# Denominators of two head pairs in one group of products, the key-query transposes of odd visits moved ahead of their scores, and another timetable for converting weights

## The chip, the cores and the metric

The kernel runs on one core of a Trainium2 chip. Its time is the device time of one execution in microseconds (us). The engines are named as in the profile: PE is TensorE (matrix products and transposes), PEld its loading of weights, DVE is VectorE, ACT is ScalarE, POOL is GpSimd, SP issues most DMAs. Each engine works through its own queue in order.

## The reference

```python
# q, k, v: (8, 12, 448, 64) f32; g_q, g_k: (64,); w_in: (768, 2048); w_out: (2048, 768)
def rmsnorm(x, g):
    return x / sqrt(mean(x * x, axis=-1) + 1e-6) * g
q_n, k_n = rmsnorm(q, g_q), rmsnorm(k, g_k)
scores = q_n @ k_n.T / 8
attn = exp(scores - max(scores)); attn = attn / (sum(attn) + 1e-9)
x = (attn @ v).transpose(0, 2, 1, 3).reshape(3584, 768)
h = maximum(x @ w_in, 0)
out = (h * h) @ w_out
```

## The kernel before

Two heads make a pair; a batch of 12 heads has 6 pairs, and 8 batches have 48, counted `i` = 0, 1, ... in order. Two pairs (an even one and the odd one behind it) share work: the 448 keys of a head are 3 slots of 128 keys and one of 64, and the last 64 keys of two pairs go together as slot `NJ` = 3.

The work around the change is **phase 1**, the visits of pairs 0 to 12 (`visit_alone(i, n)`, called for n = 0 and then n = 1). There PE does attention only. Behind it, PE's stream of FFN products begins (line L1016 first), with the attention of later pairs in between. The branch of the program used here is `shift` = False, in which exps need no shift by their maximum. Nothing is scheduled at run time: the order of instructions on every engine is that in which Python issues them, and semaphores do the waiting.

What a visit of pair i does before, by engine (lines of the kernel before):

- PE: scores of slots 0 and 1 of pair i (`score`, L449, products on 64x64 tiles, into banks 0 to 3); the **turn** of pair i+1 (`turn`, transposes of q and k by L415 and L418, q in bank 7 and k in bank 6); the values of pair i-1 for slots 0 to 2 (`attend`, L552, bank 4 for an even pair and 5 for an odd one); scores of slot 2 (L449, banks 0 and 1 again); then in an even visit the scores of the shared slot (L460, banks 2 and 3), in an odd visit the values of the shared slot for both pairs (`attend_both`, L588, the odd pair's half into bank 6); last the **sums**, the denominators of pair i-1, as products of the weights with ones (`add_weights`, L604, 16 products, four at a time side by side).
- ACT: the exps (L468) of the scores that make the weights; the squares of q (L181); the copy of k from its bank (L425); the copy of the odd pair's half, `rest` (L595); part of the conversion of FFN weights (L1696 to L1699).
- DVE: the **inversion** of pair i-2's denominators, which were summed at the end of the visit before: a transposition out of the bank (`take_sums`, L664), four small copies (L675), an addition (L676), a reciprocal (L681), a transposition back (L682); then `finish`: for an odd pair add `rest` (L715), multiply the values by the inverse (L717). For pairs of batch 1 `begin_forms` sums x into forms for the FFN (L744, on DVE and POOL in turn). Then qT of pair i+1 out of its bank (L423), and the means of squares of pair i+2, q and then k (L194, L197).
- POOL: squares of k of pair i+2 (L183), the power -1/2 of the means (L204), and the scaling of q (L219), which the next visit's turn of q waits for.
- The conversion of FFN weights: `convert` starts a piece (ACT, then DVE L1710 and L1729) at the steps in `early` (step 4i + 2n), and `make_sum` adds pieces to weight forms (L1810, one instruction on DVE, the next on POOL).

After phase 1 the sums of weights of pair 12 are added on POOL (L487) and multiplied with ones on PE (L622).

Of the kernel before, what the change touches and what calls it, by code (L numbers as in the profile page):

```python
# [14 lines left out]
F32 = mybir.dt.float32  # L15
# [4 lines left out]
ALU = mybir.AluOpType  # L20
# [3 lines left out]
P = 128  # L24


NJ = 3
NG = 2 * NJ + 1
SIDE = 32
# [196 lines left out]
def program(ctx, tc, rows, v, g, wide, ones, moe_w_in, moe_w_out, out, shift):  # L226

    nc = tc.nc

    B, H, S, D = v.shape  # L230
    NPAIR = H // 2
# [6 lines left out]
    NT = S // P  # L238
# [23 lines left out]
    banks = [psum.tile([P, 512], F32, name=f"bank{n}") for n in range(8)]  # L262
# [3 lines left out]
    pairs = [(b, c) for b in range(B) for c in range(NPAIR)]  # L266
    LASTS = S - NJ * P
# [141 lines left out]
    def turn(i, x):  # L409

        ensure("qk", i)
        tr = banks[7 - x if i < 2 or alone(i - 2) else 0]
        dst = att.tile([P, S], F32, name="qT" if x == 0 else "kT")
        for j in range(NJ):
            nc.tensor.transpose(  # L415
                tr[:, ts(j, P)], rows.part(i, x)[:, j].rearrange("p h d -> p (h d)"), ident
            )
        nc.tensor.transpose(  # L418
            tr[:, ts(NJ, P)], rows.room(i)[:, x, NJ].rearrange("p h d -> p (h d)"),
            wide[:, ds(i % 2 * LASTS, P)],  # L420
        )
        if x == 0:
            nc.vector.tensor_scalar(out=dst, in0=tr[:, 0:S], scalar1=g, scalar2=None, op0=ALU.mult)  # L423
        else:
            nc.scalar.copy(dst, tr[:, 0:S])  # L425
        turned[i, x] = dst

    def new_weights(n, e):

        i, m = n  # L430
        if m < 2 and alone(i) and not shift:
            weights[n, e] = new_acc()[:, 0:S] if m else new_part()
        else:
            weights[n, e] = att.tile([P, S], F32, name="wT", tag="wT", bufs=8)
        return weights[n, e]

    def banks_of(i, m):

# [90 lines left out]
    def values_bank(i):  # L529
        return banks[4 + i % 2 if alone(i) else 4][:, 0:S]  # L530

    def attend(i, some):

        order = values_of(i)
        for n in (i, i + 1 if i % 2 == 0 and not shift else i):
            ensure("v", n)
        for n in some:  # L540
            if n >= len(order):
                continue
            m = order[n]
            if m == NJ and not shift:
                attend_both(i)
                continue
            if joint(i):
                attend_halves(i, n)
                continue
            mine = ds(i % 2 * LASTS, LASTS) if m == NJ else ds(0, P)  # L550
            for e in range(2):
                nc.tensor.matmul(  # L552
                    values_bank(i)[ds(e * D, D), :],
                    lhsT=lasts[i % 2][mine, e, :] if m == NJ else values[i][:, m, e, :],
                    rhs=weights[key_of(i, m), e][mine], start=n == 0,
                    stop=n == len(order) - 1 and (shift or i % 2 == 1),
                )

    def second_bank(i):
        return banks[3][:, 0:S]  # L560
# [36 lines left out]
    def add_weights(i, some):  # L597

        order = sums_of(i)
        for n in some:  # L600
            m = order[n]
            mine = ds(i % 2 * LASTS, LASTS) if m == NJ and shift else ds(0, P)
            for e in range(2):
                nc.tensor.matmul(  # L604
                    sums_bank(i)[ds(e * D + n % 2 * SIDE, SIDE), :],
                    lhsT=ones_of[i % 2][mine] if m == NJ else ones[:, 0:SIDE],
                    rhs=weights[key_of(i, m), e][mine], start=n < 2, stop=n >= 2,
                )
# [53 lines left out]
    def take_sums(i):  # L662
        inverse[i] = io.tile([P, S], F32, name="inverse", tag="squares", bufs=1)
        nc.vector.transpose(inverse[i], sums_bank(i))  # L664
# [4 lines left out]
    def invert(i):  # L669
        columns = inverse[i].rearrange("p (t n) -> p t n", n=SIDE)  # L670
        few = columns[:, :, 0:1]
        if alone(i) or shift:
            other, both = new_few(), new_few()
            for n in range(P // SIDE):
                nc.vector.tensor_copy(out=other[ts(n, SIDE)], in_=few[ts(n ^ 1, SIDE)])  # L675
# [6 lines left out]
        nc.vector.transpose(columns, by.to_broadcast([P, S // SIDE, SIDE]))  # L682
# [22 lines left out]
    def finish(i):  # L705

        b, c = pairs[i]
        if joint(i):
            xT = xts[b, c]
            nc.gpsimd.tensor_tensor(out=xT, in0=xT, in1=inverse.pop(i), op=ALU.mult)  # L710
        else:
            xT = xts[b, c] = new_x()
            bank = values_bank(i)
            if i % 2 and not shift:
                nc.vector.tensor_tensor(out=xT, in0=bank, in1=rests.pop(i), op=ALU.add)  # L715
                bank = xT
            nc.vector.tensor_tensor(out=xT, in0=bank, in1=inverse.pop(i), op=ALU.mult)  # L717
        leave(i)

    def leave(i):  # L720
        b, c = pairs[i]
        scale_turned()
        for x in range(2):
            del turned[i, x]
        del values[i]
        if b == 1:
            begin_forms(c)
        elif b > 1:
            settle(b, c)
# [1129 lines left out]
    load_weights(1)  # L1859
    for i in range(2, 4):  # L1860
        rows.load(i, nc.sync)
    for n in range(2):
# [86 lines left out]
    def new_acc():  # L1949
        return keep_p.tile([P, DM], F32, name="acc", tag="acc", bufs=2 * NT + 1)  # L1950
# [30 lines left out]
    def visit_alone(i, n):  # L1981
        step = i * 2 * VISITS + 2 * n
        if n == 0:
            if i == 0:
                load_v(i)
            if i and shift:
                attend_all(i - 1)
            weigh_slots(i, n)
            turn(i + 1, 0)
            turn(i + 1, 1)  # L1990
            square(i + 2, 0, new_acc())
            square(i + 2, 1, new_acc(), nc.gpsimd)
            begin(step)
            normalize(i + 2, 0)
            if i and not shift:
                attend(i - 1, range(NJ))
        else:
            weigh_slots(i, n)
            normalize(i + 2, 1)
            begin(step)  # L2000
            if in_blocks(i + 2):
                store_q(i + 2)
                load_blocks(i + 2, 0)
                load_blocks(i + 2, 1)
            if i and not shift:
                attend(i - 1, (NJ,))
                add_weights(i - 1, range(NJ + 1))
                forget(i - 1, range(NJ + 1))
                take_sums(i - 1)
                invert(i - 1)  # L2010
                finish(i - 1)
            if i < 2 * NPAIR:
# [196 lines left out]
```

## Time and profile before

| | |
|---|---|
| median of 3 runs | 1348.09 us (1348.0 to 1348.48) |
| the profiled execution | 1348.26 us, its span 1346.5 us, TensorE clock granted 0.999 |
| phase 1 | about 17 us to 122.2 us of the span; 13 visits |
| an undisturbed visit | 8.40 us |

Busy time of the engines in stretches of the span; columns: stretch, its length, then busy time and instructions of PE, PEld, DVE, ACT, POOL, the granted clock, the DMA share and GB/s:

```profile
44.00:61.00 17.00, 17.00 (x144) 6.28 (x140) 15.21 (x37) 15.10 (x29) 12.46 (x11) 1.00 0.64 161
95.00:122.00 27.00, 25.59 (x212) 9.38 (x204) 23.46 (x50) 15.61 (x29) 19.11 (x17) 1.00 0.59 159
122.00:500.00 378.00, 376.12 (x1531) 185.44 (x1528) 280.90 (x494) 239.03 (x421) 248.28 (x213) 1.00 0.78 213
```

In a row of a timeline or of the chain the first number is the start in us from the span's start, the second the time in us. `x4` counts the instructions that the row gathers. In brackets stands how long the engine had been idle, and what released it. The visit of pair 9 starts at 87.08, that of pair 10 at 95.47, of pair 11 at 104.30, of pair 12 at 112.79. The FFN stream starts at 122.22.

### The profile page before, as it was taken

To read this page: it belongs to the slowest core of one execution; us is meant where nothing else is said; L and a number is where in the kernel's file an instruction comes from. 1 tells how busy PE (TensorE), PEld (TensorE's weight loads), DVE (VectorE), ACT (ScalarE), POOL (GpSimd) and SP (SyncE) were. 2 spreads that over 40 slices of the span, in tenths; PEclk is the share of its full clock that TensorE was granted. 3 is DMA by queue.
4 is the path that set the end of the run, shared out by engine and by line. 5 is a ranking of instruction groups with operands and counts; after the bars stand their busy time and mean duration, and the time that the engine had idled before them with its cause. 6 is when DMAs were issued, how large, how long until landed. Compare 5 with 4: busy or idle time off the path is not lost.

```text
span 1346.5 us, 21086 instructions
## 1 busy us (share of the span) xinstructions
PE 1326.0 (98%) x6988; PEld 887.2 (66%) x6988; DVE 884.0 (66%) x1739; ACT 611.4 (45%) x1135; POOL 760.6 (56%) x740
## 2 busy tenths in 40 slices
PE   7999999999999999999999999999999999999998
PEld 3333454444444486777758576676858599999998
DVE  4887866878768856465656856565655854556673
ACT  6885677768666244442434244353433134330000
POOL 5668764746556878566767878576555731110010
PEclk9999999999999999999999999999999999999999
DMA  5655965968969877574748676674737466545543
GB/s 137 156 142 131 247 187 144 283 182 219 266 149 268 255 189 221 154 219 124 234 104 251 190 186 211 169 214 119 238 83 231 145 194 196 157 132 152 161 158 101
DMA packets 416633, 245.64 MB, mean 182 GB/s; under 512 B 273284, under 2 KB 381060, under 8 KB 415492
## 3 DMA queue, kind: packets, MB, share of 16 engines
q1 hardware_dynamic: 416224, 244.15, 64.2%
q8 instruction: 57, 0.93, 0.3%
q14 instruction: 60, 0.49, 0.1%
q10 hardware_dynamic: 292, 0.07, 0.0%
HBM read 178.13 MB, written 65.99 MB: 181 GB/s over the span
## 4 chain that ended last, share of the span: by engine, by line
PE 90%; DVE 4%; DMA 2%; SPq 1%; POOL 1%; issue 1%; ACT 1%; POOLq 0%; DVEq 0%; ACTq 0%
PE bank L1077 26%; PE bank L1274 21%; PE bank L1600 9%; PE bank L1016 8%; PE bank L449 8%; PE bank L567 4%; PE bank L552 4%; PE bank L1438 2%; PE bank L460 1%; PE bank L588 1%; PE bank L604 1%; PE bank L1216 1%; PE bank L631 1%; PE bank L622 1%; DVE acc L1636 1%
## 5 line engine op out<-in xcount | busy, mean ns | idle before, releaser
L1077 PE MATMUL bank<-xT,in_sb 128*128 128x224 f32 x1344 | 287.0, 353 | 0.0
L1077 PEld LDWEIGHTS bank<-xT,in_sb 128*128 128x128 f32 x1344 | 253.1, 190 | 9.4 <-ACT wT L468 5.6
L468 ACT ACTIVATE wT<-bank,rr 128x448 f32<-128x448 f32 x288 | 163.8, 631 | 160.5 <-PE bank L449 134.9
L1274 PE MATMUL bank<-out_sb,hid 128*128 128x384 f32 x576 | 206.0, 490 | 1.7 <-DVE acc L1636 1.6
L204 POOL TENSOR_TENSOR rr<-ms,minus_half 128x8 f32<-128x8 f32 (+1 forms) x96 | 145.9, 1520 | 75.4 <-DVE ms L197 70.4
L1636 DVE TENSOR_TENSOR acc<-acc,bank 128x384 f32<-128x384 f32 x231 | 122.3, 546 | 78.7 <-PE bank L1274 58.6
L1274 PEld LDWEIGHTS bank<-out_sb,hid 128*128 128x128 f32 x576 | 107.7, 190 | 81.6 <-issue 6.6
L1274 PE MATMUL bank<-out_sb,sums 128*128 128x384 f32 x432 | 155.7, 491 | 1.1 <-DVE acc L1636 0.6
L449 PE MATMUL bank<-qT,kT 64*64 64x448 f32 x1152 | 147.0, 553 | 1.9 <-DVE qT L423 1.1
L1016 PE MATMUL bank<-xT,in_sb 128*128 128x448 f32 x336 | 129.8, 543 | 0.0
L1274 PEld LDWEIGHTS bank<-out_sb,sums 128*128 128x128 f32 x432 | 80.5, 190 | 65.5 <-issue 4.2
L487 POOL TENSOR_TENSOR sum<-sum,wT 128x448 f32<-128x448 f32 (+1 forms) x96 | 116.4, 1233 | 1.6
L1016 PEld LDWEIGHTS bank<-xT,in_sb 128*128 128x128 f32 x336 | 62.8, 190 | 66.8 <-issue 63.0
L1060 DVE TENSOR_TENSOR hid<-hid,bank 128x224 f32<-128x224 f32 x208 | 73.4, 382 | 44.3 <-PE bank L1077 41.1
L449 PEld LDWEIGHTS bank<-qT,kT 64*64 64x64 f32 x1152 | 49.5, 134 | 76.2 <-issue 50.8
L487 POOL TENSOR_TENSOR sum<-wT 128x448 f32<-128x448 f32 x48 | 56.1, 1189 | 73.1 <-ACT wT L468 66.5
L1077 PE MATMUL bank<-more,in_sb 128*128 128x224 f32 x288 | 74.4, 354 | 0.0
L567 PE MATMUL bank<-wT,vt 64*64 64x448 f32 x576 | 74.4, 545 | 0.0
L382 ACT ACTIVATE qT<-qT,g 128x448 f32<-128x448 f32 x34 | 22.5, 663 | 106.6 <-DVE qT L372 106.6
L1699 ACT ACTIVATE words<-words 128x384 f16<-128x384 f32 x64 | 68.6, 1072 | 2.0
L1547 POOL TENSOR_TENSOR acc<-acc 128x768 f32<-128x768 f32 x2 | 4.3, 2138 | 105.3 <-DVE acc L1519 105.3
L1060 DVE TENSOR_TENSOR whole_hid<-whole_hid,bank 128x224 f32<-128x224 f32 x104 | 37.7, 385 | 39.1 <-PE bank L1077 37.1
(200 smaller groups left out, 2374.7 us busy)
## 6 DMA issues: line engine op xcount, KB each, us to landing
in_sb<-in_deep SPq DMA_DIRECT2D x64, 384.0 KB, 3.8
in_sb<-in_deep SPq DMA_DIRECT2D x80, 256.0 KB, 4.3
out_sb<-out_forms SPq DMA_DIRECT2D x48, 384.0 KB, 5.6
words<-in_moe_w_in_dram SPq DMA_DIRECT2D x32, 384.0 KB, 3.9
words<-in_moe_w_out_dram SPq DMA_DIRECT2D x32, 384.0 KB, 3.5
out_forms<-out_sb SPq DMA_DIRECT2D x8, 1536.0 KB, 7.0
qk<-in_q_dram SPq DMA_DIRECT2D x96, 96.0 KB, 2.6
qk<-in_k_dram SPq DMA_DIRECT2D x96, 96.0 KB, 2.7
```

The source lines that it names most:

```text
L204: self.nc.gpsimd.tensor_tensor(out=self.rr[i][:, x, 0 : self.count(i)], in0=ms, in1=self.minus_half.to_broadcast(list(ms.shape)), op=ALU.pow,)
L449: nc.tensor.matmul(sc[ds(half * D, D)], lhsT=turned[i, 1][ds(e * D, D), ds(m * P + half * D, D)], rhs=turned[i, 0][ds(e * D, D), :], start ...
L468: nc.scalar.activation(new_weights((i, m), e), sc, AF.Exp, scale=rows.rr[i][:, 1, 2 * m + e : 2 * m + e + 1],)
L487: nc.gpsimd.tensor_tensor(out=sums[i, e][some], in0=left[some], in1=weights[key_of(i, m), e][some], op=ALU.add)
L567: nc.tensor.matmul(bank[ds(e * D, D), :], lhsT=values[i][keys, n, e, :], rhs=weights[(i, n), e][keys], start=n == 0, stop=n == NJ - 1 and ...
L1016: nc.tensor.matmul(ps, lhsT=w_sb[:, IN.index(left), c, :], rhs=forms[u, c][right], start=first and c == 0, stop=c == NK - 1, skip_group_ch ...
L1060: nc.vector.tensor_tensor(out=quarter(blk, name, n), in0=quarter(blk, base, n), in1=ps, op=ALU.add)
L1077: nc.tensor.matmul(ps, lhsT=left, rhs=right, start=start, stop=stop, skip_group_check=True)
L1274: nc.tensor.matmul(ps, lhsT=lefts[left][:, t, ts(tt, P)], rhs=w_sb[t][:, OUT.index(right), :], start=first and t == 0, stop=t == 1, skip_g ...
L1600: nc.tensor.matmul(ps, lhsT=left[l][:, blk], rhs=rest_of[r][:, blk], start=blk == 0 and product in ("P1", "P5", "P4"), stop=blk == NBLK - ...
L1636: nc.vector.tensor_tensor(out=acc, in0=acc, in1=ps, op=ALU.add)
L1699: nc.scalar.activation(sign, high.bitcast(F32), AF.Copy)
```

## The change

1. **Sums of two pairs together.** At the end of each even visit i = 2, 4, ... 12 a new function `sums_of_two` sums the denominators of the pairs i-2 and i-1 in one group in bank 6: 6 slots of 448 columns for each of the two heads, and the shared slot in halves of 224 columns. The rows of the even and the odd pair are kept apart by masks of ones and zeros in place of `ones`. A following `invert_two` inverts both pairs' denominators at once (28 columns instead of 14) and transposes back twice; `finish` for both pairs stands behind that. The weights must be kept for longer; they get room in tiles that the FFN uses later (`new_spare`, `room_for_weights`). In an odd visit the values of the even pair are copied from bank 4 (`leave_bank`), since the bank is needed.
2. **The turn first.** In odd visits, from visit 3 on, the turn of pair i+1 stands ahead of the scores of pair i, k first and in bank 4. In even visits it stays behind the scores.
3. **The timetable of conversions.** `early` was 2 + 3.1n for n = 0 to 12; it is now 2, 6, 8, 10, 16, 13, 18, 24, 26, 32, 34, 40, 42, that is mostly two conversions in an even visit. (13 stands behind 16, so it is done in visit 4, which has three.)

```diff
+    def turned_first(i):
+        return i % 2 == 0 and 2 < i <= 2 * NPAIR and not shift
...
-        tr = banks[7 - x if i < 2 or alone(i - 2) else 0]
+        tr = banks[4 if x and turned_first(i) else 7 - x if i < 2 or alone(i - 2) else 0]
...
+    def sums_of_two(i):
+        bank = banks[6][:, 0:S]
+        ones_for = spare[14]
+        for n in range(2 * NJ + 1):
+            p, m = divmod(n, NJ) if n < 2 * NJ else (0, NJ)
+            for e in range(2):
+                some = weights.pop(((i + p, m), e))
+                if m < NJ:
+                    nc.tensor.matmul(
+                        bank[ds(e * D + n % 2 * SIDE, SIDE), :], lhsT=ones_for[p], rhs=some,
+                        start=n < 2, stop=False, skip_group_check=True,
+                    )
+                    continue
+                for half in range(2):
+                    columns = ts(half, S // 2)
+                    nc.tensor.matmul(
+                        bank[ds(e * D + half * SIDE, SIDE), columns], lhsT=ones_for[2],
+                        rhs=some[:, columns], start=False, stop=True, skip_group_check=True,
+                    )
+        inverse[i] = io.tile([P, S], F32, name="inverse", tag="squares", bufs=1)
+        nc.vector.transpose(inverse[i], bank)
+        inverse[i + 1] = spare[10]
+
+    def invert_two(i):
+        columns = [inverse[i + p].rearrange("p (t n) -> p t n", n=SIDE) for p in range(2)]
+        few = columns[0][:, :, 0 : SIDE : SIDE // 2]
+        other, both, by = spare[11:14]
+        for n in range(P // SIDE):
+            nc.vector.tensor_copy(out=other[ts(n, SIDE)], in_=few[ts(n ^ 1, SIDE)])
+        nc.vector.tensor_tensor(out=both, in0=few, in1=other, op=ALU.add)
+        nc.vector.reciprocal(out=by, in_=both)
+        for p in range(2):
+            nc.vector.transpose(
+                columns[p], by[:, :, p : p + 1].to_broadcast([P, S // SIDE, SIDE])
+            )
+
+    def leave_bank(i):
+        xT = xts[pairs[i]] = new_x()
+        nc.vector.tensor_copy(out=xT, in_=values_bank(i))
+        del values[i]
...
+        elif (b, c) in xts:
+            xT = xts[b, c]
+            nc.vector.tensor_tensor(out=xT, in0=xT, in1=inverse.pop(i), op=ALU.mult)
...
-    early = deque(2 + 3.1 * n for n in range(ahead - tile_pieces + 1))
+    early = deque([2, 6])
+    early.extend(8 * n + 2 * m for n in range(1, NPAIR) for m in range(2))
+    early.insert(5, 13)
...
-            weigh_slots(i, n)
-            turn(i + 1, 0)
-            turn(i + 1, 1)
+            if turned_first(i + 1):
+                turn(i + 1, 1)
+                turn(i + 1, 0)
+                weigh_slots(i, n)
+            else:
+                weigh_slots(i, n)
+                turn(i + 1, 0)
+                turn(i + 1, 1)
...
-            if i and not shift:
+            if i % 2 and not shift:
                 attend(i - 1, (NJ,))
-                add_weights(i - 1, range(NJ + 1))
-                forget(i - 1, range(NJ + 1))
-                take_sums(i - 1)
-                invert(i - 1)
+                leave_bank(i - 1)
+            elif i and not shift:
+                sums_of_two(i - 2)
+                invert_two(i - 2)
+                finish(i - 2)
                 finish(i - 1)
```

In PE's order, from the third scores of an odd visit to the turn of the even visit behind it (bank_178 to bank_181 are banks 0 to 3, bank_184 is bank 6, bank_185 is bank 7; each row gives the line, the operation, out<-in, the shape and a count), there stood before:

```order
L449 MATMUL bank_178<-qT,kT 64x448 x2
L449 MATMUL bank_179<-qT,kT 64x448 x2
L588 MATMUL bank_182<-wT,lasts_162 64x448 x2
L588 MATMUL bank_184<-wT,lasts_163 64x448 x2
L604 MATMUL bank_183<-part,ones 32x448 x2
L604 MATMUL bank_183<-acc,ones 32x448 x2
L604 MATMUL bank_183<-wT,ones 32x448 x2
L604 MATMUL bank_183<-wT,ones_of_164 32x448 x2
L449 MATMUL bank_178<-qT,kT 64x448 x2
```

and stands now:

```order
L491 MATMUL bank_178<-qT,kT 64x448 x2
L491 MATMUL bank_179<-qT,kT 64x448 x2
L674 MATMUL bank_182<-wT,lasts_162 64x448 x2
L674 MATMUL bank_184<-wT,lasts_163 64x448 x2
L491 MATMUL bank_178<-qT,kT 64x448 x2
L491 MATMUL bank_179<-qT,kT 64x448 x2
L491 MATMUL bank_180<-qT,kT 64x448 x2
L491 MATMUL bank_181<-qT,kT 64x448 x2
L419 MATMUL bank_185<-wide,qk_65 128x128 x3
```

The sums are gone from between two scores into the same banks 0 and 1 (L491 is L449 of before, L674 is L588, L419 is L415).

In DVE's order, the odd visit of pair 9 began before with the inversion and finish of one pair (pair 7):

```order
L664 STREAM_TRANSPOSE inverse<-bank_182 128x448
L675 COPY few<-inverse 32x14 x4
L676 TENSOR_TENSOR few<-inverse,few 128x14
L681 RECIPROCAL few<-few 128x14
L682 STREAM_TRANSPOSE inverse<-few 128x448
L715 TENSOR_TENSOR xT<-bank_183,rest 128x448
L717 TENSOR_TENSOR xT<-xT,inverse 128x448
L744 TENSOR_TENSOR xT<-xT 128x448
L423 TENSOR_SCALAR qT<-bank_185,g 128x448
L194 TENSOR_REDUCE ms<-acc 128x6
```

and begins now with those of two (pairs 6 and 7; L799 is the even pair's multiply, L806 the odd pair's, L833 a step of the forms of x, L427 the copy of qT):

```order
L622 STREAM_TRANSPOSE inverse<-bank_184 128x448
L631 COPY sums<-inverse 32x28 x4
L632 TENSOR_TENSOR sums<-inverse,sums 128x28
L633 RECIPROCAL sums<-sums 128x28
L635 STREAM_TRANSPOSE inverse<-sums 128x448
L635 STREAM_TRANSPOSE sums<-sums 128x448
L799 TENSOR_TENSOR xT<-xT,inverse 128x448
L833 TENSOR_TENSOR xT<-xT 128x448
L804 TENSOR_TENSOR xT<-bank_183,rest 128x448
L806 TENSOR_TENSOR xT<-xT,sums 128x448
L833 TENSOR_TENSOR xT<-xT 128x448
L427 TENSOR_SCALAR qT<-bank_185,g 128x448
```

The copy of qT and the means of squares behind it stand behind a longer row of work.

In POOL's order around the visits 10 and 11 there stood before:

```order
L219 TENSOR_TENSOR qk_64<-qk_64,rr 128x512
L1810 TENSOR_TENSOR out_sb<-out_sb 128x384
L204 TENSOR_TENSOR rr<-ms,minus_half 128x8
L744 TENSOR_TENSOR xT<-xT 128x448 x2
L183 TENSOR_TENSOR acc<-qk_64 128x384
L204 TENSOR_TENSOR rr<-ms,minus_half 128x6
L219 TENSOR_TENSOR qk_64<-qk_64,rr 128x384
```

and stands now:

```order
L219 TENSOR_TENSOR qk_64<-qk_64,rr 128x512
L204 TENSOR_TENSOR rr<-ms,minus_half 128x8
L833 TENSOR_TENSOR xT<-xT 128x448 x2
L1899 TENSOR_TENSOR out_sb<-out_sb 128x384
L183 TENSOR_TENSOR acc<-qk_64 128x384
L204 TENSOR_TENSOR rr<-ms,minus_half 128x6
L219 TENSOR_TENSOR qk_64<-qk_64,rr 128x384
```

A sum of weight forms (L1810, now L1899) has moved behind the two form steps of x, between them and the squares, the power and the scaling of q of pair 13 (L219), which the turn in visit 12 needs.

More of the change, by code (lines that the diff above doesn't have):

```diff
@@ L430, in new_weights @@
         i, m = n
-        if m < 2 and alone(i) and not shift:
-            weights[n, e] = new_acc()[:, 0:S] if m else new_part()
+        if m < NJ and alone(i) and not shift:
+            weights[n, e] = room_for_weights(i, m, e)
+        elif m == 1 and i == 2 * NPAIR and not shift:
+            weights[n, e] = new_acc()[:, 0:S]
         else:
@@ L435, in new_weights, with new_spare, room_for_weights @@
         return weights[n, e]
+    spare = []
+    def new_spare():
+        for a in range(2):
+            some = hidden_p.tile([P, 2, 2, S], F32, name="hid", tag=f"hid{a}", bufs=1)
+            spare.extend(some[:, n // 2, n % 2] for n in range(4))
+        some = [
+            hidden_p.tile([P, 2, NT * P], F32, name="sums", tag=f"S{n}", bufs=1).rearrange(
+                "p t n -> p (t n)"
+            ) for n in range(3)
+        ]
+        spare.extend(x[:, 0:S] for x in some)
+        more = some[2][:, S : 2 * NT * P]
+        for n in range(3):
+            spare.append(more[:, ts(n, 2 * S // SIDE)].rearrange("p (t n) -> p t n", n=2))
+        half = SIDE // 2
+        masks = more[:, 6 * S // SIDE : 6 * S // SIDE + 5 * half]
+        nc.gpsimd.memset(masks, 0.0)
+        nc.gpsimd.memset(masks[:, ts(1, half)], 1.0)
+        for n in range(2):
+            nc.gpsimd.memset(masks[ds(n * LASTS, LASTS), ts(3 + n, half)], 1.0)
+        spare.append([masks[:, ds(n * half, SIDE)] for n in (1, 0, 3)])
+    def room_for_weights(i, m, e):
+        if i % 4 == 0 or i == 2 * NPAIR - 1:
+            return spare[2 * m + e]
+        if m == 0:
+            return new_part()
+        if i % 2 == 0:
+            return spare[4 + 2 * m + e]
+        if m == 1:
+            return new_acc()[:, 0:S]
+        return att.tile([P, S], F32, name="wT", tag="wT", bufs=8)
     def banks_of(i, m):
@@ L724, in leave @@
             del turned[i, x]
-        del values[i]
+        values.pop(i, None)
         if b == 1:
@@ L1861, in program @@
         rows.load(i, nc.sync)
-    for n in range(2):
+    if not shift:
+        new_spare()
+    for n in range(2 if shift else 0):
         nc.gpsimd.memset(ones_of[n][ds((1 - n) * LASTS, LASTS)], 0.0)
```

3 lines of the change are left out of this document (added).

## Prediction

> **What bounds the kernel now.** I read the page's busy table first, then the chain that ended last over the first 130 us (phase 1), then the timelines of the engines there.
>
> ```profile
> span 1346.5 us, 21086 instructions
> PE 1326.0 (98%) x6988; PEld 887.2 (66%) x6988; DVE 884.0 (66%) x1739; ACT 611.4 (45%) x1135; POOL 760.6 (56%) x740
> ```
>
> PE is busy 98% of the span: an edit gains only by shortening PE's stream and loses only by making PE wait. One visit of phase 1 (an odd one) in the chain:
>
> ```profile
> 53.36 1.66 PE bank L449 x16
> ...
> 56.05 2.40 PE bank L552 x12
> 58.45 0.91 PE bank L449 x8
> 59.37 0.75 PE bank L588 x8
> 60.12 1.64 PE bank L604 x16
> ```
>
> A visit is scores 1.66, turn 56.05-55.02 = 1.03 (53.36+1.66 = 55.02), values 2.40, third scores 0.91, the odd visit's second half of the third values 0.75, sums 1.64: 8.40 with no gap. Nothing but PE stands in this chain: DVE, ACT and POOL have slack here, and the question is how much.
>
> **PE's own work.** L588 follows L449 in the same tile shape, so its 8 products are two rounds of four: 0.375 a round. L449's 16 products are four rounds and 1.66 - 1.50 = 0.16 over, L604's four rounds and 0.14: a change of tile shape is about 0.16. Per two visits the change takes one round of sums away (14 products' time and two halves are 7 rounds, 8 before) and two changes of shape (one sums group instead of two; the even visit's scores stand right behind the odd visit's third values, both of 64x64 tiles). That is 0.375 + 2 x 0.16 = 0.69, for six groups **-4.14**. Bounds: -2.25 if no change of shape is saved, -4.5 with changes of 0.19; I take the middle, which the rows give.
>
> Two of the waits that PE has now go as well, since the turns they hold move or are released differently:
>
> ```profile
> 106.06 0.55 PE L415 MATMUL bank<-wide,qk 128*128 128x128 f32 x3 [0.45 <-POOL qk L219]
> ...
> 115.49 0.55 PE L415 MATMUL bank<-wide,qk 128*128 128x128 f32 x3 [0.96 <-POOL qk L219]
> ```
>
> **-1.41** (from 0, if they merely move, to that).
>
> From here T is the start of the turn in an odd visit, now the visit's first work. Without a wait PE takes 1.03 + 1.66 + 2.40 + 1.66 (third scores and third values) + 1.50 (the even visit's scores), so the even visit's turn could start at T+8.25. That is the number to compare with; before it was 8.40 + 1.66 = 10.06 behind the start of the odd visit.
>
> **Wait A: the exps.** The even visit's scores need banks 0 and 1, which ACT's exps of the odd visit's third scores read. Before, turn, values and sums of other work stood between; now only the third values (0.75) do.
>
> ```profile
> 24.78 0.98 PE L449 MATMUL bank<-qT,kT 64*64 64x448 f32 x8
> ...
> 25.80 1.16 ACT L468 ACTIVATE wT<-bank,rr 128x448 f32<-128x448 f32 x2 [1.13 <-PE bank L449]
> ```
>
> The exps start 25.80 - 24.78 = 1.02 behind the scores and both end 1.16 later. Third scores start at T+5.09, so the exps are done at 7.27, the second tiles' weights load at 7.32, and four rounds with their change (1.66) end at **8.98**: +0.73 in each of six even visits, 4.4 in all, which by itself eats the gain. Bounds: 0 (were the banks others) to 0.73.
>
> **Wait B: DVE's chain, then POOL, then the turn.** The even visit's turn needs q of pair i+2 scaled on POOL, for which DVE sums the squares, behind the whole inversion on its in-order queue. An odd visit of before, whose scores start at 87.08 (so 87.26 is +0.18):
>
> ```profile
> 87.26 0.65 DVE L664 STREAM_TRANSPOSE inverse<-bank 128x448 f32<-128x448 f32 x1 [0.42 <-PE bank L604]
> 87.95 0.72 DVE L675 COPY few<-inverse 32x14 f32<-32x14 f32 x4
> ...
> 89.19 0.65 DVE L682 STREAM_TRANSPOSE inverse<-few 128x448 f32<-128x448 f32 x1
> 89.76 0.59 DVE L715 TENSOR_TENSOR xT<-bank,rest 128x448 f32<-128x448 f32 x1
> 90.38 0.62 DVE L717 TENSOR_TENSOR xT<-xT,inverse 128x448 f32<-128x448 f32 x1
> 91.04 0.62 DVE L744 TENSOR_TENSOR xT<-xT 128x448 f32<-128x448 f32 x1
> 91.58 0.68 DVE L423 TENSOR_SCALAR qT<-bank,g 128x448 f32<-128x448 f32 x1
> 92.18 0.54 DVE L194 TENSOR_REDUCE ms<-acc 128x6 f32<-128x384 f32 x1
> ```
> ```profile
> 93.00 1.36 POOL L204 TENSOR_TENSOR rr<-ms,minus_half 128x6 f32<-128x6 f32 x1 [2.56 <-DVE ms L197]
> 94.44 0.83 POOL L219 TENSOR_TENSOR qk<-qk,rr 128x384 f32<-128x384 f32 x1
> ```
>
> New chain: first transposition at 0.18 + 1.93 (87.26 to 89.19) = T+2.11, second at 2.68 (0.57, as 89.19 to 89.76), the even pair's multiply 3.25, the odd pair's addition 3.91 (0.66, as 90.38 to 91.04), its multiply 4.53 (0.62), qT 5.19. From qT to the end of the scaling it was 94.44 + 0.83 - 91.58 = 3.69, so 8.88, and with 0.05 for the handover the turn at **8.93**: as late as A makes it. 28 columns instead of 14 in the short operations I cost at nothing (these are mostly fixed time; at most as much again, 0.7). But this is the bare chain, and four visits have more in it.
>
> Slower copies: with POOL at work beside them the four copies took
>
> ```profile
> 96.32 1.62 DVE L675 COPY few<-inverse 32x14 f32<-32x14 f32 x4
> ...
> 114.63 1.37 DVE L675 COPY few<-inverse 32x14 f32<-32x14 f32 x4
> ```
>
> 0.65 to 0.90 over 0.72; I take 0.77. POOL's other work:
>
> ```profile
> 76.25 1.00 POOL L1810 TENSOR_TENSOR in_sb<-in_sb 128x384 f32<-128x384 f32 x1 [2.65 <-DVE in_sb L1810]
> ```
> ```profile
> 109.77 2.69 POOL L744 TENSOR_TENSOR xT<-xT 128x448 f32<-128x448 f32 x2 [1.22 <-DVE xT L717]
> 112.42 0.82 POOL L183 TENSOR_TENSOR acc<-qk 128x384 f32<-128x384 f32 x1
> 113.21 1.32 POOL L204 TENSOR_TENSOR rr<-ms,minus_half 128x6 f32<-128x6 f32 x1
> 114.60 0.83 POOL L219 TENSOR_TENSOR qk<-qk,rr 128x384 f32<-128x384 f32 x1
> ```
>
> Even visits' turns, by the new order of DVE and POOL (start, and wait over 8.25):
> - Visit 2: no inversion yet; A alone, 8.98: 0.73.
> - Visit 4: A still, 8.98: 0.73 (slow copies would make it 1.45).
> - Visit 6: POOL is late with sums of weight forms from visit 4's three conversions, the copies run beside it: 8.93 + 0.77 = 9.70: 1.45.
> - Visit 8: a form sum stands ahead of qT on DVE (0.55, an estimate from 91.04 to 91.58), ends at 5.74; POOL's form sum waits for it and stands ahead of the squares (1.00 + 0.82), another form sum (1.00), power and scaling (113.21 to 115.43 less the gap, 2.27): 10.9: 2.65.
> - Visit 10: two form steps of x (L744's kind, 0.54 each) ahead of qT: 8.93 + 1.09 = 10.02: 1.77.
> - Visit 12: the odd pair's multiply ends at 4.53 + 0.54 + 0.66 = 5.72; POOL's two form steps wait for it (2.69), then a form sum (1.00), then squares, power, scaling as above (112.46 to 115.43, 2.97): 12.5: 4.25.
>
> Sum **+11.58**. Low bound 4.4 (A alone); high bound: visit 4 with slow copies, and 0.7 for wider operations in five visits, 15.8. I take the middle because the order gives each step and every length is a row.
>
> **The end of phase 1.** After visit 12 POOL has form steps of two pairs, four instead of two, ahead of the sums of weights of pair 12, for which PE waits already:
>
> ```profile
> 122.22 4.78 PE L1016 MATMUL bank<-xT,in_sb 128*128 128x448 f32 x12
> ...
> 137.21 1.01 PE L622 MATMUL bank<-sum,ones 128*64 128x448 f32 x4
> ```
> ```profile
> 127.09 2.69 POOL L744 TENSOR_TENSOR xT<-xT 128x448 f32<-128x448 f32 x2 [1.21 <-DVE xT L717]
> 129.74 2.21 POOL L487 TENSOR_TENSOR sum<-wT 128x448 f32<-128x448 f32 x2
> 131.92 5.28 POOL L487 TENSOR_TENSOR sum<-sum,wT 128x448 f32<-128x448 f32 x4
> ```
>
> POOL's sums end at 137.20 and PE's product starts at 137.21, no slack. The form steps ended 129.78 - 122.22 = 7.56 behind the start of the stream; now the first may start behind the even pair's multiply (3.25 + 0.62 + 0.05 = 3.92) and four take 5.38: 9.33 with the handovers. **+1.77** (0 if PE finds cover, to 2.69).
>
> **Costed at nothing:** the conversions' ACT work and kT's copy (ACT idles 1.13 in the row above), the copy of the even pair's values out of bank 4 (one DVE operation more per odd visit, behind the squares), the masks (POOL, before PE starts), the DMAs (their number and order stay). If DVE's copy were on the path, 0.6 per odd visit.
>
> **Sum.** -4.14 - 1.41 + 11.58 + 1.77 = +7.8. The profiled execution took 1348.26 (span and 1.76 around it), 0.17 over the median of the runs: 1348.26 + 7.8 - 0.17 = **1355.9**. Own range 1351.9 to 1358.5: half of B's excess (-4), or the wider operations in part (+2.6).
>
> **A rule weighed.** The row first: the product of two SBUF tiles took 0.77 beside POOL's squares and 0.62 above.
>
> ```profile
> 57.51 0.77 DVE L717 TENSOR_TENSOR xT<-xT,inverse 128x448 f32<-128x448 f32 x1
> ```
>
> The Trainium skill, "GPSIMD Engine Reference", section "1. Specifications", says that GpSimd shares its SBUF interfaces with VectorE and contends with DVE instructions that read two SBUF inputs or run in a 2-port mode. The trace agrees by 0.15 here and by the slow copies. By it the two multiplies of visit 5's chain would be held too, about 0.8 more in all (an estimate from these rows): 1356.7.
>
> **Rivals.**
> - *Waits hidden: faster.* If POOL's scaling ends before T+8.25 in every visit and the exps are early, the gain stays whole: 1348.09 - 4.14 = 1344.0, 1342.5 with both old waits gone. For: POOL idled 2.56 ahead of its power. Against: that idling is a wait for DVE's chain, now longer; the scaling would have to end 0.68 earlier at least and A vanish. Chance 0.12.
> - *A alone: no change.* If the chain stays within A, 4.4 - 4.14, with or without -1.41: 1347 to 1348.4; with the end, 1350. For: bare 8.93 against 8.98. Against: visits 8, 10 and 12. Chance 0.12.
> - *It does not do what it says.* No change of shape is saved, so PE's gain is 2.25: 1357.8. Against: L588 without excess. Chance 0.06.
> - *All contention adds up,* 4 more: 1360. Chance 0.08.
> - The forecast: 0.62.
>
> The smallest difference that counts is 0.2%, 2.7 us. Slower 0.62 + 0.06 + 0.08 = 0.76, no change 0.12, faster 0.12. The range 1348.0 to 1360.0 leaves out the faster rival and the last's upper half, 0.16.
>
> **What would show it.** Right: PE idle ahead of the turn in even visits, released by POOL's scaling, about 2 in visits 8 and 10 and near 4 in visit 12; loads of the even visits' scores waiting for ACT's exps; the FFN stream starting at about 128 instead of 122.2; the sums seven rounds, 2.77. Wrong: turns at T+8.3 with no idle ahead; the scaling of q ending well before; PE's wait at the end of phase 1 covered by other products. The likeliest way to be wrong: a visit that PE enters late gives DVE and POOL time to catch up, so that the waits do not add up visit by visit.

## The result and the profile after

The changed kernel takes 1364.61 us (median of 4 runs, 1362.64 to 1366.1), the kernel before 1348.05 (4 runs): 1.0121 times as long, 95% interval 1.0105 to 1.0137. The forecast was 1355.9, with a range up to 1360. The direction was right; the loss is 16.5 where 7.8 was forecast.

The page of the profiled execution of the changed kernel (1364.61 us):

```profile
span 1362.4 us, 21034 instructions
PE 1331.1 (98%) x6988; PEld 890.0 (65%) x6988; DVE 876.8 (64%) x1703; ACT 613.2 (45%) x1135; POOL 760.5 (56%) x740
```

PE has as many instructions as before and is busy 5 us *longer*, though the change takes work away from it. A part of that is wait A, which stands inside a group of scores and counts as busy there; with wait A and a full clock in phase 1, PE is busy 1327.1 (e1 below). The other 4 mean that products themselves take longer. PE's timeline of the visits 7 and 8 (T = 71.65 is the turn in visit 7):

```profile
71.65 0.55 PE L419 MATMUL bank<-wide,qk 128*128 128x128 f32 x3
...
78.45 2.24 PE L491 MATMUL bank<-qT,kT 64*64 64x448 f32 x16
82.57 0.55 PE L419 MATMUL bank<-wide,qk 128*128 128x128 f32 x3 [1.87 <-POOL qk L219]
...
83.59 1.56 PE L594 MATMUL bank<-part,vt 128*64 128x448 f32 x4
84.93 1.71 PE L594 MATMUL bank<-acc,vt 128*64 128x448 f32 x4
86.42 1.34 PE L594 MATMUL bank<-wT,vt 128*64 128x448 f32 x4
87.69 0.98 PE L491 MATMUL bank<-qT,kT 64*64 64x448 f32 x8
```

The scores at 78.45 take 2.24 instead of 1.66 (wait A, inside the group). Then PE idles for POOL's scaling of q (wait B), and the turn comes at T+10.92. What the forecast did not have follows: the values (L594) take 87.69 - 83.59 = 4.10 instead of 2.40. Stretches of 10 and 20 us tell why (stretch, length, busy times of PE, PEld, DVE, ACT and POOL, granted clock, DMA share, GB/s):

```profile
80.00:90.00 10.00, 8.13 (x50) 2.83 (x48) 5.54 (x11) 6.06 (x12) 8.16 (x8) 0.83 0.41 97
90.00:110.00 20.00, 18.65 (x164) 7.38 (x156) 13.02 (x29) 16.11 (x30) 9.86 (x9) 1.00 0.51 124
120.00:130.00 10.00, 6.72 (x40) 2.54 (x36) 4.80 (x11) 3.16 (x7) 8.77 (x9) 0.83 0.52 191
150.00:160.00 10.00, 9.05 (x33) 3.09 (x34) 6.73 (x13) 5.02 (x10) 9.72 (x9) 0.83 0.92 244
```

The granted clock fell behind each of PE's three longest waits. Of the rows of values above, the second takes 86.42 - 84.93 = 1.49 until the next begins; at the full clock this is 0.75 (85.36 - 84.61 in e5 below), so the clock is halved for a time, and 0.83 is the mean of a stretch. The longest wait is in visit 12 (PE, then DVE and POOL ahead of it):

```profile
118.64 1.73 PE L491 MATMUL bank<-qT,kT 64*64 64x448 f32 x16 [1.76 <-DVE qT L427]
123.65 0.55 PE L419 MATMUL bank<-wide,qk 128*128 128x128 f32 x3 [3.27 <-POOL qk L219]
```
```profile
115.86 0.62 DVE L833 TENSOR_TENSOR xT<-xT 128x448 f32<-128x448 f32 x1
116.41 1.49 DVE L1899 TENSOR_TENSOR out_sb<-out_sb 128x384 f32<-128x384 f32 x1
117.82 0.67 DVE L427 TENSOR_SCALAR qT<-bank,g 128x448 f32<-128x448 f32 x1
```
```profile
115.91 2.98 POOL L833 TENSOR_TENSOR xT<-xT 128x448 f32<-128x448 f32 x2 [5.45 <-DVE xT L806]
118.85 1.31 POOL L1899 TENSOR_TENSOR out_sb<-out_sb 128x384 f32<-128x384 f32 x1
120.12 1.14 POOL L183 TENSOR_TENSOR acc<-qk 128x384 f32<-128x384 f32 x1
121.37 1.32 POOL L204 TENSOR_TENSOR rr<-ms,minus_half 128x6 f32<-128x6 f32 x1
122.77 0.83 POOL L219 TENSOR_TENSOR qk<-qk,rr 128x384 f32<-128x384 f32 x1
```

POOL does exactly the row of work that the forecast named: form steps behind the odd pair's multiply, a form sum, squares, power, scaling. DVE's form sum beside it took 1.49; in visit 7, with POOL idle, the same kind took 0.55.

Behind phase 1 PE waits for POOL's sums of weights, which the four form steps delay:

```profile
133.21 4.78 PE L1105 MATMUL bank<-xT,in_sb 128*128 128x448 f32 x12
...
150.70 0.97 PE L708 MATMUL bank<-sum,ones 128*64 128x448 f32 x2 [2.43 <-POOL sum L529]
151.91 0.85 PE L708 MATMUL bank<-sum,ones 128*64 128x448 f32 x1 [0.25 <-POOL sum L529]
```
```profile
137.23 6.09 POOL L833 TENSOR_TENSOR xT<-xT 128x448 f32<-128x448 f32 x4 [6.04 <-DVE xT L799]
143.28 2.78 POOL L529 TENSOR_TENSOR sum<-wT,acc 128x448 f32<-128x448 f32 x2
146.02 5.83 POOL L529 TENSOR_TENSOR sum<-sum,wT 128x448 f32<-128x448 f32 x4
```

The FFN stream starts at 133.21 instead of 122.22, 10.99 later; the rest of the span's 15.9 is lost within the next 25 us, and from there the kernels run alike.

### The profile page after: what moved, and what is told of

Its sections match the earlier page's. It is cut to its first block, busy times and chain, and to the rows that moved or that the text cites. A ratio compares the mean times of both kernels' runs of the same rounds, so it can differ in the third digit from the quotient of the medians.

```text
span 1362.4 us, 21034 instructions
## 1 busy us (share of the span) xinstructions
PE 1331.1 (98%) x6988; PEld 890.0 (65%) x6988; DVE 876.8 (64%) x1703; ACT 613.2 (45%) x1135; POOL 760.5 (56%) x740
## 4 chain that ended last, share of the span: by engine, by line
PE 68%; DVE 3%; DMA 1%; issue 1%; SPq 0%; ACT 0%; POOL 0%; DVEq 0%; ACTq 0%; POOLq 0%
PE bank L1166 26%; PE bank L1363 17%; PE bank L1689 9%; PE bank L491 5%; PE bank L653 4%; PE bank L1105 2%; PE bank L1527 2%; PE bank L502 1%; PE bank L717 1%; PE bank L674 1%; PE bank L594 1%; DVE acc L1725 1%; DMA qk<-in_k_dram 0%; DMA words<-in_moe_w_in_dram 0%; DVE acc L833 0%
## 5 line engine op out<-in xcount | busy, mean ns | idle before, releaser
L510 ACT ACTIVATE wT<-bank,rr 128x448 f32<-128x448 f32 x272 | 155.3, 631 | 162.6 <-PE bank L491 140.6
L491 PE MATMUL bank<-qT,kT 64*64 64x448 f32 x1152 | 148.9, 552 | 4.0 <-DVE qT L427 3.2
L1105 PE MATMUL bank<-xT,in_sb 128*128 128x448 f32 x336 | 129.8, 543 | 0.0
L1105 PEld LDWEIGHTS bank<-xT,in_sb 128*128 128x128 f32 x336 | 62.8, 190 | 66.4 <-issue 62.5
L491 PEld LDWEIGHTS bank<-qT,kT 64*64 64x64 f32 x1152 | 51.1, 133 | 76.7 <-issue 48.2
```

The source lines that it names most:

```text
L491: nc.tensor.matmul(sc[ds(half * D, D)], lhsT=turned[i, 1][ds(e * D, D), ds(m * P + half * D, D)], rhs=turned[i, 0][ds(e * D, D), :], start ...
L510: nc.scalar.activation(new_weights((i, m), e), sc, AF.Exp, scale=rows.rr[i][:, 1, 2 * m + e : 2 * m + e + 1],)
L1105: nc.tensor.matmul(ps, lhsT=w_sb[:, IN.index(left), c, :], rhs=forms[u, c][right], start=first and c == 0, stop=c == NK - 1, skip_group_ch ...
```

## The experiments

Theory: DVE's longer chain and POOL behind it make the even visits' turns late (B); PE's waits then cost clock as well. Rivals: ACT's exps (A) decide alone; the turn first, or the new timetable, makes the loss; the clock falls for reasons of its own. All kernels start from the changed one.

**e1, DVE's order.** In odd visits the copy of qT ahead of the inversion's copies (the transposition out of the bank stays ahead of it), finish of the odd pair, form steps and form sums behind q's means of squares:

```diff
                 turn(i + 1, 0)
+                invert_two(i - 3)
+                finish(i - 3)
                 weigh_slots(i, n)
...
-            begin(step)
+            if i % 2 == 0 or i < 3 or shift:
+                begin(step)
             normalize(i + 2, 0)
+            if i % 2 and i >= 3 and not shift:
+                finish(i - 2)
+                begin(step)
...
```

At the end of the even visit the same calls (`invert_two`, `finish` twice) now stand only for the last one, visit 12.

> The changed kernel, with DVE's queue in odd visits in another order: the copy of qT first, then the inversion of both denominators and the even pair's multiply, then q's means of squares, and only behind them the odd pair's finish, the form steps and the sums of weight forms. Theory (DVE's chain, then POOL, makes the even visits' turns late, and two waits of PE over 1.8 us halve the granted clock for some 4 us): the even visits' turns start about 9.0 behind the odd ones in visits 6 to 12 instead of 10.04, 10.92, 10.06 and 13.60, visit 4 about 9.5; no loss of clock in phase 1; the FFN stream starts 12 us earlier, at about 121; the wait behind phase 1 for POOL's sums of weights stays; total 1352 to 1353. Rival (the waits are ACT's, by the exps alone): no change, 1363 to 1366. Rival (the granted clock falls for another reason than PE's waits): the turns as above, but the clock of about 0.95 in phase 1 stays, 1356.

Measured: 1352.99 (ratio to before 1.0041, interval 1.0028 to 1.0054), 11.6 off the loss by moving instructions on DVE and POOL alone. The turns of visits 6, 8, 10 and 12 came 9.48, 8.97, 9.00 and 9.34 behind the odd ones, no stretch of phase 1 had a clock below 1.00, the FFN stream started at 121.61. B, with the clock that its waits cost, is shown as the main cause.

**e2, the banks.** Slots 0 and 1 exchange banks in even visits:

```diff
-        return [banks[m % 2 * 2 + e][:, 0:S] for e in range(2)]
+        swap = i % 2 == 0 and 0 < i <= 2 * NPAIR and m < 2 and not shift
+        return [banks[(m + swap) % 2 * 2 + e][:, 0:S] for e in range(2)]
```

> The changed kernel, where even visits of phase 1 put the scores of slot 0 into banks 2 and 3 and those of slot 1 into banks 0 and 1, so that they don't wait for the exps of the odd visit's third scores. Theory (DVE and POOL decide from visit 6 on): only visits 2 and 4 gain, 0.7 each at most; total 1363 to 1365. Rival (ACT's exps decide in all even visits): 0.73 in each of six visits, 1360; with them the loss of clock may go as well, 1357.

Measured: 1364.24 (1.0120, 1.0104 to 1.0135): nothing that can be told from the changed kernel. While B holds the turns, A is hidden behind it: the turns of visits 6 to 12 come 10.05, 10.91, 10.24 and 13.58 behind the odd ones, as in the changed kernel. The trace of e2 also holds a case that speaks against a simple rule for the clock. With A gone, PE idles 2.58 ahead of visit 8's turn, longer than the 1.87 of the changed kernel, and the clock does not fall; the values behind it take 85.88 - 83.47 = 2.41:

```profile
82.45 0.55 PE L419 MATMUL bank<-wide,qk 128*128 128x128 f32 x3 [2.58 <-POOL qk L219]
...
83.47 0.97 PE L595 MATMUL bank<-part,vt 128*64 128x448 f32 x4
...
85.88 0.98 PE L492 MATMUL bank<-qT,kT 64*64 64x448 f32 x8
```
```profile
80.00:90.00 10.00, 7.55 (x64) 3.08 (x68) 5.42 (x11) 7.57 (x14) 8.15 (x8) 1.00 0.51 121
```

**e3, both.**

> Both edits at once: DVE's order of the first and the banks of the second. Theory: with the chain out of the way the exps are the wait that is left, 0.73 in each even visit; without it the even visits' turns start 8.25 to 8.4 behind the odd ones, phase 1 ends at 117 to 118, total about 1348.5 to 1349.5, the wait behind phase 1 left. Rival (the exps hide nothing): the same as the first kernel, 1352 to 1353.

Measured: 1351.64 (1.0029, 1.0018 to 1.0040): a miss. The turns came 8.82 to 9.39 behind the odd ones, now released by POOL's scaling (waits of 0.2 to 1.0): B, shortened, ends just where A did. Taking either away shows the other.

**e4 and e5, PE kept busy.** Products that nobody reads, into bank 7 ahead of its transposes, in the waits of visits 8 and 12; 5 and 8 of them in e4, 2 and 4 in e5:

```diff
                 weigh_slots(i, n)
+                for _ in range({8: 2, 12: 4}.get(i, 0)):
+                    nc.tensor.matmul(
+                        banks[7][:, 0:S], lhsT=ident, rhs=turned[i, 0], start=True, stop=True
+                    )
                 turn(i + 1, 0)
```

> The changed kernel with more work: 5 products of 448 columns (about 2 us) ahead of the turn in visit 8 and 8 (about 3.1 us) ahead of that in visit 12, into bank 7 before the transposes overwrite it; nobody reads them. They fill PE's two longest waits. Theory (PE's idle time halves the granted clock afterwards): the clock stays at 1.00 in phase 1, the values behind these two turns take 2.4 instead of 4.1 each, and the kernel is faster with more work: 3.4 less, about 1361. Rival (the clock falls for another reason, or these waits cost only their own length): no gain, 1364 to 1366.

> The changed kernel with unread products into bank 7 again, but sized by what the fourth run showed, 0.76 us for one of 448 columns on the whole array: 2 ahead of the turn in visit 8 (1.5 us in a wait of 1.87) and 4 ahead of that in visit 12 (3.0 us in 3.27), so that no turn starts later. Theory (PE's idle time lowers the clock): the clock stays 1.00 in phase 1, the FFN stream starts 3.4 earlier than in the changed kernel, at 129.8, and the total is about 1361. Rival (the wait costs only its own length): 1364 to 1366, as with more products.

Measured: e4 1365.10. Its clock stayed at 1.00, but one product took 0.76, not the 0.4 assumed, so that the turns came 1.9 and 2.8 later behind the odd ones (12.86 and 16.41) and ate the gain. e5, sized to fit, 1362.16 (1.0110, 1.0095 to 1.0126), 2.45 below the changed kernel by the medians, 3.5 by the profiled spans. PE's timeline of e5 and its stretch (each product has two rows in the profile, so the 2 unread ones are x4):

```profile
80.81 1.77 PE L2089 MATMUL bank<-qT,wide 128*128 128x448 f32 x4
82.78 0.55 PE L419 MATMUL bank<-wide,qk 128*128 128x128 f32 x3 [0.20 <-POOL qk L219]
...
83.81 0.97 PE L594 MATMUL bank<-part,vt 128*64 128x448 f32 x4
84.61 0.92 PE L594 MATMUL bank<-acc,vt 128*64 128x448 f32 x4
85.36 0.92 PE L594 MATMUL bank<-wT,vt 128*64 128x448 f32 x4
86.21 0.98 PE L491 MATMUL bank<-qT,kT 64*64 64x448 f32 x8
```
```profile
80.00:90.00 10.00, 9.80 (x72) 3.73 (x70) 5.72 (x12) 7.76 (x15) 8.15 (x8) 1.00 0.49 116
```

The turn of visit 8 comes as late as without (T+10.94), yet the values take 86.21 - 83.81 = 2.40. More work, less time. By the totals this is not quite clear of noise: the slowest of e5's four runs (1363.65) lies above the fastest of the changed kernel's (1362.64). The granted clocks leave no overlap: 0.996 or 0.997 in all four runs of the changed kernel, 0.998 to 1.000 in all eight of e4 and e5. So it is PE's idling that costs the clock, though not every time, as e2 shows.

**e6, the old timetable** (`early = deque(2 + 3.1 * n ...)` again).

> The changed kernel with the old timetable of conversions (2 + 3.1n). Theory: without the form sums in the odd visits' chains on DVE and POOL, visit 12's turn comes about 10 to 10.5 behind visit 11's instead of 13.60, the second loss of clock goes, visit 8's stays late since conversions stand ahead of qT there; total about 1358 to 1360. Rival (the two pairs' inversion alone makes the loss): 1363 to 1366. Rival (the new table is needed): slower than 1367.

Measured: 1361.83 (1.0101, 1.0085 to 1.0116), less of a gain than expected. Visit 12's turn came 11.55 behind instead of 13.60, and its wait of 2.48 cost no clock; visit 4's got worse (10.37 for 9.50). The timetable is some 3 of the 16.5.

**e7, the turn not first** (`turned_first` returns False).

> The changed kernel with the turns of odd visits behind their scores again, k in bank 6. Theory: the even visit's turn can start 8.25 behind the start of the odd visit either way, and DVE's chain, which decides, has the same length; total 1362 to 1366. Rival (the turn first makes the loss): the waits of the even visits shrink by the scores' 1.66 each, below 1358.

Measured: 1364.43 (1.0117, 1.0102 to 1.0133), as expected: this part of the change costs and brings nothing that these times can tell.

**e8, more moved behind.** The even pair's multiply behind q's means too, and the last form steps on DVE:

> The banks and the order of the third run, and two more edits: in odd visits the even pair's multiply and form step also stand behind q's means of squares on DVE; and the last form steps of x (pairs 10 and 11) run on DVE instead of POOL, so that POOL begins its sums of weights behind phase 1 sooner. Theory: the even visits' turns come 8.3 to 8.6 behind the odd ones (8.8 to 9.4 in the third run), the FFN stream starts at 117.5 to 118.5, PE's wait for POOL's sums behind it shrinks from 1.9 to nothing: 1344 to 1346, faster than both kernels. Rival (what is left of the waits is not DVE's chain): 1350 to 1352, as the third run.

Measured: 1351.02 (1.0025, 1.0015 to 1.0036): a miss. The turns came 8.63 to 9.43 behind, and behind phase 1 PE waited for the odd pair's addition (L805), ahead of which three of DVE's six form steps stood:

```profile
130.59 7.03 PE L1107 MATMUL bank<-xT,in_sb 128*128 128x448 f32 x18 [1.52 <-DVE xT L805]
```

**e9, q scaled first.** Besides e2's banks:

```diff
                 turn(i + 1, 0)
+                square(i + 2, 0, new_acc())
+                normalize(i + 2, 0)
+                invert_two(i - 3)
+                finish(i - 3)
+                finish(i - 2)
                 weigh_slots(i, n)
...
```

The same calls no longer stand where they stood before.

**e10** adds four form steps on DVE behind both multiplies; **e11** is e10 with the old banks.

> The changed kernel with the banks of the second run and another order in odd visits: ACT squares q of pair i+2 right behind the copy of k, ahead of the exps; DVE takes the copy of qT, then q's means of squares, and only then the inversion; POOL's power and scaling of q come ahead of all its other work of the visit. Theory (the scaling of q, whatever holds it, makes the even visits' turns late): POOL ends the scaling some 5 to 6 behind the odd visit's start, the even visits' turns come 8.25 to 8.4 behind the odd ones (visit 4 up to 8.8 for the copy of k), the FFN stream starts at 117 to 118, and with PE's wait for POOL's sums still there the total is 1345 to 1346. Rival (something else than q's scaling keeps 0.6 in each of these visits): the stream starts at 120 to 121, total 1350 to 1351.

> The kernel of the ninth run, with the four last form steps of x that POOL had moved to DVE, behind both pairs' multiplies. Theory: POOL's sums of weights behind phase 1 start as early as before, PE's wait of about 2 for them goes, and DVE's four more operations (2.5) fall into its idle time; 1343 to 1344, faster than both kernels. Rival (DVE's work is late instead, as in the eighth run): as the ninth, 1345 to 1346.

> The kernel of the tenth run without the exchange of banks. Theory: with q's scaling out of the way the exps are the wait that shows, and the even visits' turns come 8.98 behind the odd ones: 0.6 to 0.7 more in each of six visits, 3.5 to 4.4 more than the tenth run, about 1347. Rival (the exps never decided anything): the same as the tenth run.

Measured: e9 1351.48 (1.0024, 1.0014 to 1.0033), e10 1348.74 (1.0006, 0.9997 to 1.0015), e11 1351.33 (1.0022, 1.0012 to 1.0032). The totals of e9 and e10 miss by 5 and that of e11 by 4 (e11 is 2.6 behind e10, 3.5 to 4.4 were expected); in the visits 8 to 12 the mechanism is what was expected. Two turns that follow each other, of e10 and then of e11:

```profile
86.88 0.55 PE L419 MATMUL bank<-wide,qk 128*128 128x128 f32 x3
...
95.14 0.55 PE L419 MATMUL bank<-wide,qk 128*128 128x128 f32 x3
```
```profile
88.90 0.55 PE L419 MATMUL bank<-wide,qk 128*128 128x128 f32 x3
...
97.90 0.33 PE L419 MATMUL bank<-wide,qk 128*128 128x128 f32 x1
```

8.26 without A and B (8.25 in the forecast), 9.00 with A alone (8.98). The rest of the miss stands elsewhere: in e9 and e10 visit 5's turn waits 1.5 for a q that POOL scales late, visit 4 having three conversions (e12 has two there and no such wait), and in visit 11 DVE's form sums are slow beside POOL and DVE then waits for POOL's squares (DVE, then POOL, of e10):

```profile
111.04 2.91 DVE L1909 TENSOR_TENSOR out_sb<-out_sb 128x384 f32<-128x384 f32 x2
114.67 0.55 DVE L194 TENSOR_REDUCE ms<-acc 128x6 f32<-128x384 f32 x1 [0.72 <-POOL acc L183]
```
```profile
110.54 2.99 POOL L842 TENSOR_TENSOR xT<-xT 128x448 f32<-128x448 f32 x2 [2.72 <-DVE xT L809]
113.50 1.14 POOL L183 TENSOR_TENSOR acc<-qk 128x384 f32<-128x384 f32 x1
```

e10 also settles what the form steps on POOL cost behind phase 1: from the stream's start to PE's products with the sums of weights it takes 14.99, as before the change, and 16.95 in e9. But what e10 gains there is lost later: at 398.68 PE waits 1.39 for DVE's transposition (L751), and in the profiled execution the clock is 0.69 from 400 to 405, some 1.7 more. e8 has the same wait of 1.39 and no loss of clock.

**e12, these two mended:** k's squares ahead of the forms, step 13 back in visit 3 (`early.insert(4, 13)`), pair 10's last form steps on DVE, pair 11's on POOL.

> The kernel of the ninth run with three more edits: POOL's squares of k also ahead of the forms in odd visits (in the tenth run DVE waited for them behind POOL's form steps, and visit 12's last scores for DVE); the conversion of step 13 back in visit 3, so that visit 4 has two (its third made visit 5's turn of q wait 1.5); and of the last four form steps that POOL had, pair 10's on DVE behind both multiplies, pair 11's on POOL as before. Theory: the waits of the tenth run at visits 5, 6 and 12 go (1.5 + 0.2 + 1.2), DVE's inversion behind phase 1 is late by half as much (1.4 before), the FFN stream starts at 117 to 118; total 1344 to 1346, faster than both kernels by more than 2. Rival (the waits move on to other operations, as they did from the third run to the eighth): 1348 to 1350, the same as before.

Measured: 1348.75 against 1348.47 (1.0005, 0.9996 to 1.0014): no difference, as the rival had it. Phase 1 is now faster: the FFN stream starts at 119.61, 2.6 earlier than before. But the sums of weights are not (PE, then POOL):

```profile
135.87 0.97 PE L709 MATMUL bank<-sum,ones 128*64 128x448 f32 x2 [1.20 <-POOL sum L530]
137.29 0.59 PE L709 MATMUL bank<-sum,ones 128*64 128x448 f32 x1 [0.45 <-POOL sum L530]
...
139.74 0.93 PE L492 MATMUL bank<-qT,kT 64*64 64x448 f32 x8
```
```profile
125.46 3.06 POOL L836 TENSOR_TENSOR xT<-xT 128x448 f32<-128x448 f32 x2 [3.92 <-DVE xT L809]
128.48 3.05 POOL L530 TENSOR_TENSOR sum<-wT,acc 128x448 f32<-128x448 f32 x2
131.49 5.74 POOL L530 TENSOR_TENSOR sum<-sum,wT 128x448 f32<-128x448 f32 x4
```

POOL ends at 137.23, where it ended before (137.20), and both kernels do the scores behind it at the same time (139.74 and 139.71). What phase 1 gains, PE waits for POOL. No version that beats the kernel before was found. e12's phase 1 with e10's end, where that wait was gone and the later one of 1.39 for DVE had come, was not tried.

## Why the prediction was right and wrong

Right, to a tenth: PE's own gain (from an even turn to the next odd one the forecast's terms leave 16.80 - 0.69 - 8.25 = 7.86, and 7.86 to 7.87 were measured where the clock is full; from odd to even 8.25 were forecast and 8.26 measured in e10), wait A (8.98; 9.00 in e11), and the mechanism of B in visits 8, 10 and 12. The even visits' turns behind the odd ones:

| visit | forecast | changed kernel |
|---|---|---|
| 4 | 8.98 | 9.50 |
| 6 | 9.70 | 10.04 |
| 8 | 10.9 | 10.92 |
| 10 | 10.02 | 10.06 |
| 12 | 12.5 | 13.60 |

Ahead of visit 4's turn PE waited 0.46 (at 39.60, in visit 3) for ACT's copy of k, which "costed at nothing" had hidden behind idle time of another visit. Visit 6 comes near its number partly by luck: the slow copies that were to make it late took 0.90 and not 1.49, and instead a conversion on DVE (L1818, 1.44 from 53.61) held the first transposition until T+1.22. In visit 12 POOL's own row was slower, 2.98 for 2.69, 1.31 for 1.00 and 1.14 for 0.82, which is 0.9 of the 1.1. DVE's form sums, slow at the same time, add nothing to it: q's means ended at 121.28, POOL's squares at 121.26. Together the five turns come 2.0 later than forecast.

Wrong, and the step that failed: the **sum** added up waits as if each cost its own length. Behind the waits in visits 8 and 12 the values took 4.10 instead of 2.40, which is 3.4 in phase 1, and behind the third wait another 1.4 or so (from L1105 at 133.21 to the shared values it took 21.72, in e4 with the same wait and a full clock 20.33). That term of 4.8 is missing, and e5 shows it. The Trainium skill, "TensorE: Matmul & The Clock Gate", section "Part 1: The HAM clock gate (the "warmup" mystery)", states it: the clock is halved after an idle window of about 3.4 us, and a busy window of that length restores it. The trace agrees with the halving (1.49 for 0.75) and with the length of the loss (1.7 lost at half the clock are 3.4 at it, an estimate from these rows), but the waits that cost it were shorter, 1.87 and 2.43 besides 3.27. Nor does length alone decide. Of the waits of PE of 1.87 to 3.28 between 17 and 165 us of the kept traces, 11 are followed by a loss and 6 are not: 1.89 in e1 and 1.90 in e3 cost none and 1.89 in e9 did; 2.42 in e4 and e5 cost none and 2.43 in the changed kernel did. The same page of the Trainium skill calls its window free-running, so that it need not begin with the wait; this might explain why equal waits differ, but not how a wait shorter than the window costs anything. No run here tests it, and the cause of the difference stays open.

Mis-sized: **the end of phase 1**, 1.77 forecast. From the stream's start to the shared values behind POOL's sums it took 16.69 before and 21.72 after, 5.0 more, of which 1.4 is clock. The form steps took 6.09, not 5.38, and the sums 8.61, not 7.49: POOL was slower beside a DVE that was now at work at the same time, with its own finish and then with form sums. Without the clock's part the end of phase 1 is 3.6, 1.9 more than forecast. The three misses, 4.8 of clock, 2.0 in the turns and 1.9 here, make up the 8.7 between the forecast and the result.

The rule weighed in the prediction, on contention between VectorE and GpSimd (the Trainium skill, "GPSIMD Engine Reference", section "1. Specifications"), was applied to instructions that hardly met POOL, and the 0.8 that was worked out from it is more than its rows give (twice 0.15). The two multiplies of visit 5 took 0.69, beside POOL's squares, and 0.63, with POOL almost idle. Where one ran beside POOL's form steps it was held: 0.91 at 138.38, behind phase 1. DVE's form sums, which also read two SBUF inputs, were held in visit 11 (1.49 for 0.55; in e10 two of them 2.91 beside POOL's 2.99).

## What to carry to other kernels

An engine that is off the critical path has a due time; when it gets more work ahead of what the busy engine waits for, the order in its queue decides, and not its load (e1 and e9 took most of the loss back without one instruction less). Price a wait on TensorE by more than its length: one of about 2 us can cost 1.7 more in clock, and in one trace a wait of 1.39 did too. It does not always, so look at the granted clock by stretch before blaming a wait or clearing it. When work is grouped so that it comes later (two pairs in one group), look where the last group's results are due: what phase 1 gained was lost at the next wait, which stood ready with no slack.

## What the hardware showed unexpectedly

TensorE's granted clock can fall after an idle time of only 1.87 us (0.83 over the 10 us around it), and in e10 after 1.39, while 1.76 in visit 12's scores left the products that followed at full speed (1.73 for the 16), and so did 2.58 in e2. Where unread products filled the gap (e4, e5), it did not fall. And two engines that work on SBUF side by side slow each other: DVE's 0.55 became 1.49, POOL's pair of form steps 2.69 became 2.98 to 3.06.
